# Start of an attention and expert kernel written in place, ranks in six products, first expert split later

## The chip, the cores and the metric

The program runs on one core of a Trainium2 chip. The metric is the device time of one execution in microseconds (us). The core has five engines, each with its own queue of instructions in a fixed order: TensorE (PE, matmuls), VectorE (DVE), ScalarE (ACT), GpSimd (POOL) and SyncE (SP, which mostly issues DMAs). They wait for each other through semaphores. An instruction that waits holds up everything behind it on its own engine.

## What is computed

Attention over 8 batches of 8 heads with 576 tokens and a head size of 64, in which scores below the row maximum less tau are dropped, and then a layer of 8 experts of which each token takes the best one:

```python
scores = scale * np.matmul(q, k.transpose(0, 1, 3, 2))
thresh = np.max(scores, axis=-1, keepdims=True) - tau
scores = np.where(scores >= thresh, scores, -1000000000.0)
attn = np.exp(scores - np.max(scores, axis=-1, keepdims=True))
attn = attn / (np.sum(attn, axis=-1, keepdims=True) + 1e-09)
x = np.matmul(attn, v)            # transposed to [4608, 512]
logits = x @ w_gate
expert_idx = np.argmax(logits, axis=1)
gate_w = softmax(logits)[np.arange(N), expert_idx]
for e in range(8):                # xe: the tokens of expert e
    out[expert_idx == e] = gate_w[mask, None] * (np.maximum(xe @ w1[e], 0.0) @ w2[e])
```

All in float32: q, k, v [8, 8, 576, 64], w1 [8, 512, 1024], w2 [8, 1024, 512].

## The kernel before

**Precision.** float32 operands are held as two float16 parts, `hi` (the rounded value) and `lo` (the rest), and a product takes two or three float16 matmuls.

**Pairs and steps.** The 64 heads are worked on as 32 pairs, 10 steps to a pair. In step k, `s_unit` (L276) computes a tile of scores s of a pair that is ten steps ahead, from which DVE takes row maxima (nm, L298). `parts(n)` (L301) joins these into r, PE transposes r (tile pst, L309), ACT and DVE split the result into three float16 rows (ptT, L314 to L317), and three DMAs write these rows into the operand tile CQ (L323). `st_unit` (L325) computes the transposed scores st with that CQ, so that the threshold is already subtracted; ACT takes the exponential, DVE masks it, ACT and POOL split it into ph and pl, and `av_piece` (L393) multiplies by v a pair later.

**Operands of a pair.** `load_qk` (L207) loads q and k of a pair as one tile of 128 partitions (a head in each half), `split` (L215) makes hi and lo, and `stack` (L230) copies their halves with 12 DMAs on SP (L243 to L252) into the tiles QK, ck and CQ that the matmuls read; in these the halves of the 128 partitions hold different parts of the same head. At the start this is also done for pairs 0, 1 and 2, before the first threshold rows.

**Routing.** When a batch b is done, its rows are transposed by DMAs (xTg, L499), `logits` (L513) multiplies by the gate, DVE finds the best expert, and `ranks` (L569) counts each token's place within its expert, by matmuls of 8 columns. A chain on DVE (rk to posi, L581 to L588) ends in row numbers, by which POOL sends the rows to the buffer xs (L596). The functions `tables0` to `tables2` (L1000 on) build the lists of rows for each expert (a DVE chain, all at L619, that ends in the tile `row`); `fetch` (L808) gathers rows with them (Rm, L816), and DMAs on SP transpose these (xTm, L822). `pst`, `lg`, `rk` and the tables' `pc` all use one PSUM tile (the pool `ps_m` has one buffer), so that the matmul of one waits until the one before has been read.

**Experts.** `load_w` (L763) loads 512 KB of weights on SP, `split_w` (L776) makes their hi on ACT (L782) and lo on DVE (L783), eight such pieces to an expert. The first expert has two load buffers; piece i + 2 is loaded when piece i has been split. `gemm1` (matmul L874) and `gemm2` (matmul L901) are cut into chunks, of which 0.15 of a chunk runs in each step from 304 to 320, and one in each step after.

**What sets the order.** Functions are planned for a step (`plan`, `after`), and each step writes out what is due. From `first` (step -20) to step 304 (KM) the instructions stand on every engine as they are written; the start ahead of it (loads, constants, the first pair) and everything from step 304 on are put in order by a scheduler. Before, the first expert's eight pieces are split in steps 286, 289 and so on to 307 (L1058 to L1060):

```python
    k = NSTEP * (NPAIR - 2) - LEAD - SL
    plan(k + 1, room)
    for i in range(8):
        plan(k + WS0 + WSD * i, lambda i=i: split_w(*wseq[i]))
```

## Time and profile before

| | |
|---|---|
| device time of three runs, us | 975.71, 977.86, 980.07 (median 977.86) |
| the profiled execution, us | 975.46 |
| its span, first to last instruction, us | 973.4 (2.1 lie outside it) |
| mean granted clock of TensorE in it | 0.986 |
| busy, us (share of the span) | PE 919.6 (94%), DVE 646.3 (66%), ACT 618.6 (64%), POOL 558.7 (57%) |

A profile tells for each engine when it was busy, and for its idle stretches which other engine's event or DMA ended them. The granted clock says at which part of full speed PE ran: 1.00 is 2.4 GHz, 0.50 is 1.2 GHz. Attention takes the first 571 us; what follows are the other experts.

### The profile page before, as it was taken

The page shows a single profiled execution, that of the slowest core. Times are in us where ns is not written, and L with a number is a line of the kernel's source. Part 1 is how long each engine was busy: PE and PEld are TensorE (multiplying, and loading weights), DVE is VectorE, ACT ScalarE, POOL GpSimd, SP SyncE. Part 2 cuts the span into 40 slices and gives each one's busy share as a digit, 9 for nine tenths or more (in the row PEclk, how much of TensorE's full clock was granted, in tenths as well). Part 3 has the DMA queues.
Part 4 walks back from the last instruction along what each step waited for, and adds up shares of the span by engine and source line. Part 5 has one row for each costly group of instructions (what it writes and reads, how often), then busy time and mean ns, then how long its engine had stood idle before and what let it go on. Part 6 is the DMA issues. An engine that isn't in the chain of part 4 may idle for free. (4 is left out here: it accounts for less than half of the span.)

```text
span 973.4 us, 25204 instructions
## 1 busy us (share of the span) xinstructions
PE 919.6 (94%) x10027; PEld 653.2 (67%) x10027; DVE 646.3 (66%) x1309; ACT 618.6 (64%) x1036; POOL 558.7 (57%) x477
## 2 busy tenths in 40 slices
PE   3699999999999999999988999899999999999997
PEld 1267777676777767767656787586677666677684
DVE  6698888888888888888888755735243341532650
ACT  2589898888888988988867744335333342433651
POOL 5378887998998979989957743431222212121121
PEclk9899999999999999999988999999999999999999
DMA  7554565484675765936656579998475565646720
GB/s 184 135 123 106 126 145 136 121 184 115 181 154 138 168 139 137 206 96 160 141 147 175 97 196 308 341 201 238 141 230 155 177 171 155 221 124 212 227 95 27
DMA packets 181715, 158.96 MB, mean 163 GB/s; under 512 B 137561, under 2 KB 153947, under 8 KB 181596
## 3 DMA queue, kind: packets, MB, share of 16 engines
q1 hardware_dynamic: 129244, 100.35, 42.2%
q10 hardware_dynamic: 43200, 27.53, 10.8%
q0 software_dynamic: 9152, 29.45, 9.2%
q8 instruction: 80, 1.31, 0.6%
q14 instruction: 39, 0.32, 0.1%
HBM read 90.24 MB, written 19.44 MB: 113 GB/s over the span
## 5 line engine op out<-in xcount | busy, mean ns | idle before, releaser
L372 POOL TENSOR_TENSOR pl<-e,ph 128x1024 f16<-128x1024 f32 x95 | 203.0, 2139 | 61.9 <-ACT ph L371 58.6
L298 DVE TENSOR_REDUCE nm<-s 128x1 f32<-128x512 f32 (+1 forms) x320 | 202.0, 635 | 16.6 <-PE s L288 13.5
L901 PE MATMUL y<-wb,hl 128*128 128x512 f16 (+1 forms) x1056 | 201.5, 360 | 1.3 <-DVE hl L863 1.3
L874 PEld LDWEIGHTS <-wb 128*128 128x128 f16 x2304 | 188.6, 98 | 19.9 <-issue 2.4
L874 PE MATMUL h<-xTm,wb 128*128 128x256 f16 (+2 forms) x2112 | 195.5, 253 | 1.8 <-DMA xTm<-R 1.8
L901 PEld LDWEIGHTS <-hl 128*128 128x128 f16 (+1 forms) x1056 | 94.1, 100 | 100.5 <-DVE hl L863 2.3
L783 DVE SCALAR_TENSOR_TENSOR wb<-wf,wb 128x1024 f16<-128x1024 f32 x96 | 118.6, 1269 | 56.6 <-ACT wb L782 55.0
L366 DVE SCALAR_TENSOR_TENSOR e<-st,e 128x512 f32<-128x512 f32 x192 | 129.3, 674 | 37.2 <-POOL pl L372 25.7
L363 ACT ACTIVATE e<-st,ntau 128x512 f32<-128x512 f32 x192 | 129.9, 688 | 36.9 <-PE st L336 35.0
L286 PE MATMUL s<-QK 128*128 128x512 f16 (+3 forms) x640 | 137.5, 293 | 13.9 <-DMA QK<-lo 13.6
L288 PE MATMUL s<-ck,CQ 128*128 128x512 f16 (+3 forms) x640 | 142.1, 290 | 3.3 <-DMA ck<-lo 3.3
L335 PE MATMUL st<-QK 128*128 128x512 f16 (+3 forms) x640 | 138.1, 292 | 3.2 <-DVE e L366 3.0
L336 PE MATMUL st<-CQ,ck 128*128 128x512 f16 (+3 forms) x640 | 132.7, 290 | 7.2 <-DMA CQ<-ptT 7.2
L915 POOL DMA_INDIRECT out_dram<-o,gt x40 | 43.6, 1089 | 133.6 <-ACT o L912 123.0
L782 ACT ACTIVATE wb<-wf 128x1024 f16<-128x1024 f32 x96 | 97.2, 1048 | 33.0 <-DMA wf<-in_w_dram 18.0
L414 PE MATMUL av<-vf,e 128*128 128x65 f32 (+1 forms) x1024 | 116.9, 252 | 0.0
L862 ACT ACTIVATE hl<-h 128x512 f16<-128x512 f32 (+1 forms) x80 | 45.8, 572 | 111.6 <-PE h L874 109.5
L347 ACT ACTIVATE e<-st,ntau_f 128x512 f32<-128x512 f32 (+1 forms) x160 | 94.4, 611 | 28.7 <-PE st L336 28.5
L414 PEld LDWEIGHTS av<-vf,e 128*128 128x128 f32 (+1 forms) x1024 | 102.1, 165 | 0.3
L371 ACT CAST ph<-e 128x1024 f16<-128x1024 f32 x96 | 99.4, 1036 | 3.5 <-DVE ptT L317 1.6
L418 PE MATMUL av<-vop,pl 128*128 128x65 f16 x768 | 97.5, 195 | 0.0
L417 PE MATMUL av<-vop,ph 128*128 128x64 f16 x768 | 97.4, 194 | 0.0
(203 smaller groups left out, 1490.7 us busy)
## 6 DMA issues: line engine op xcount, KB each, us to landing
wf<-in_w_dram SPq DMA_DIRECT2D x96, 512.0 KB
qkf<-in_qk_dram ACTq DMA_DIRECT2D x30, 576.0 KB
vf<-in_v_dram ACTq DMA_DIRECT2D x30, 320.0 KB
QK<-hi SPq DMA_DIRECT2D x64, 144.0 KB
QK<-hi SPq DMA_DIRECT2D x64, 72.0 KB
QK<-lo SPq DMA_DIRECT2D x64, 72.0 KB
ck<-lo SPq DMA_DIRECT2D x64, 72.0 KB
CQ<-hi SPq DMA_DIRECT2D x64, 64.0 KB
```

The source lines that it names most:

```text
L286: nc.tensor.matmul(sc[rows, oc], d["QA"][a][:, cols], d["KB"][a][:, CH[c]], start=True, stop=False)
L288: nc.tensor.matmul(sc[rows, oc], d["CQ"][:, at:at + cols.stop - cols.start], d["CK"][a][:, CH[c]], start=False, stop=True,)
L298: nc.vector.tensor_reduce(o, sc[:, 0:width(t)], axis=AX.X, op=ALU.max, negate=True)
L335: nc.tensor.matmul(sc[rows, oc], d["KB"][a][:, cols], d["QA"][a][:, CH[c]], start=True, stop=False)
L336: nc.tensor.matmul(sc[rows, oc], d["CK"][a][:, cols], d["CQ"][:, q], start=False, stop=True)
L363: nc.scalar.activation(pf, sc, AF.Exp, bias=ntau, scale=0.125 / SS)
L366: nc.vector.scalar_tensor_tensor(pf, sc, 0.0, pf, ALU.is_ge, ALU.mult)
L372: (nc.vector if (n, t) in PLV else nc.gpsimd).tensor_tensor(l, pd, h, ALU.subtract)
L414: nc.tensor.matmul(av[rows, a], d["Pf"][t][:, q], vf[:, tv], start=False, stop=last)
L783: nc.vector.scalar_tensor_tensor(o[:, :, 1], x, SW, o[:, :, 0], ALU.mult, ALU.subtract)
L874: nc.tensor.matmul(o, Wt[:, c, wh, f], x, start=c == 0 and z == 0, stop=c == 3 and z == 2,)
L901: nc.tensor.matmul(o, h[:, hh], Wt[:, f, wh, c], start=f == 0 and z == 0, stop=f == 7 and z == 2)
```

## The change

- **Start.** The order written by hand begins with the first instruction. Pair 0 is loaded twice, so that each half of the 128 partitions holds the same head (four DMAs on SP), and ACT, DVE and POOL write QK, ck and CQ of it in place (`rounded_0`, `rest_0`): its 12 copies by DMA are gone. Pair 1 is loaded on ACT's queue, split by ACT and POOL, and its 12 copies stand half on SP and half on ACT. Pair 2 is split sooner, its copies in the order hi, CQ, lo. The threshold rows of pair 0 go out on ACT's queue. Constants that nobody needs yet (iotas, memsets, the gate's weights) are held back and written five to a step on POOL and two to a step on DVE; the fourth buffer's memsets move from DVE to POOL.
- **Ranks.** A batch of n blocks takes n + 1 matmuls of up to 8 n columns in place of n (n + 3) / 2 of 8 columns: six for n = 5 (20 before), five for n = 4 (14 before).
- **First expert.** Its pieces are split in steps 300, 302, 304, 306, 309, 312, 315 and 318.
- **Logits of batch 6.** They move from step 306 to step 315, with a dependency on the last matmul of st.

```diff
--- before.py
+++ after.py
@@ start of the program, inside the order that is written by hand @@
+    for a in range(2):
+        for z in range(2):
+            nc.sync.dma_start(xds[a][64 * z:64 * z + 64], qk[0][64 * a:64 * a + 64])
+    for i in range(3):
+        fill(i, nc.vector)
+        nc.gpsimd.memset(cqs[i][64:P], 0.0)
+        if i == 0:
+            nc.scalar.copy(hqs[0][64:P, 0:1], cks[0][0][64:P, 0:1])
+            for w in range(2):
+                nc.scalar.dma_start(x1[w], qk[1][:, w])
+
+    def rounded_0(a):
+        nc.scalar.activation(hqs[a], xds[a][:, 0], AF.Copy, scale=SQ)
+        nc.scalar.activation(qks[a][:, 1], xds[a][:, 1], AF.Copy, scale=SQ)
+
+    def rest_0(a):
+        q, k = xds[a][LO, 0], xds[a][HI, 1]
+        nc.vector.scalar_tensor_tensor(qks[a][LO, 0], q, SQ, hqs[a][LO], ALU.mult, ALU.subtract)
+        nc.vector.scalar_tensor_tensor(cks[0][a][HI], k, SQ, qks[a][HI, 1], ALU.mult, ALU.subtract)
+        nc.gpsimd.tensor_copy(qks[a][HI, 0], hqs[a][HI])
+        copy = nc.gpsimd.tensor_copy if a else nc.scalar.copy
+        copy(cqs[0][HI, a * NT * P:(a + 1) * NT * P], hqs[a][HI, 0:NT * P])
+        copy(cqs[0][HI, 8 * P + 64 * a:8 * P + 64 * a + 64], hqs[a][HI, NT * P:S])
...
-    nc.gpsimd.iota(iota_i, pattern=[[1, E]], base=0, channel_multiplier=0)
+    hg.iota(iota_i, pattern=[[1, E]], base=0, channel_multiplier=0)
...
+    for w in range(2):
+        nc.scalar.activation(hi_1[:, w], x1[w], AF.Copy, scale=SQ)
+    for w in range(2):
+        nc.scalar.activation(x1[w], x1[w], AF.Copy, scale=SQ)
+        nc.gpsimd.tensor_tensor(lo_1[:, w], x1[w], hi_1[:, w], ALU.subtract)
...
+    def spread():
+        for eng, k0, w in ((hg, 3, 5), (hv, 13, 2)):
+            for i, f in enumerate(eng.ops):
+                plan(first + k0 + i // w, f)
@@ stack(n) @@
+        if n == 1:
+            for h, e in ((x, nc.sync), (y, nc.scalar)):
+                for f in first(*h) + query(*h) + low(*h):
+                    f(e)
+            return
+        if n == 2:
+            for part in first, query, low:
+                for h in heads:
+                    for f in part(*h):
+                        f(nc.sync)
+            return
@@ parts(n), rows(t) @@
-                nc.sync.dma_start(
+                (nc.sync if n else nc.scalar).dma_start(
@@ finish(b): step of the logits @@
-            d + TUNE["lg7"] if last else phase(7, d + TUNE["lg"]), lambda: logits(b, n, xTs, dist),
+            d + TUNE["lg7"] if last else phase(7, d + (14 if b == B - 2 else TUNE["lg"])), lambda: logits(b, n, xTs, dist),
...
+                if b == B - 2 and j == m == 0:
+                    tc.add_manual_dep(mm.ins, mark[0].name, SYNC)
@@ ranks() @@
-            for j in range(n):
-                nc.tensor.matmul(rkv[:, j], before, oh[:, j], start=True, stop=False)
-                for i in range(j):
-                    nc.tensor.matmul(rkv[:, j], ones, oh[:, i], start=False, stop=False)
-                nc.tensor.matmul(rkv[:, j], ones, was, start=False, stop=True)
+            nc.tensor.matmul(rkv, before, oh, start=True, stop=False)
+            for i in range(n - 1):
+                nc.tensor.matmul(
+                    rkv[:, i + 1:n], ones, oh[:, i:i + 1].to_broadcast([P, n - 1 - i, E]), start=False, stop=False
+                )
+            nc.tensor.matmul(rkv, ones, was.unsqueeze(1).to_broadcast(bc), start=False, stop=True)
@@ plans of the pairs and of the first expert @@
-            plan(max(first, k - TUNE["sp0"]), lambda n=n: split(n))
-            plan(max(first + 3, k), lambda n=n: stack(n))
+            plan(max(first + 3, k) if n > 1 else first + 2, lambda n=n: stack(n))
...
-        plan(k + WS0 + WSD * i, lambda i=i: split_w(*wseq[i]))
+        k = KEND - 2 * NSTEP + 2 * i + max(i - 3, 0)
+        plan(k, lambda i=i: split_w(*wseq[i]))
```

**SP at the start.** The threshold rows of pair 0 (`CQ<-ptT`, L323 before) stand behind the last copies of pair 2. QK, ck and CQ are the stacked operands, hi and lo the parts of a pair. Before:

```order
L243 DMA QK_1_360<-hi_307 64x1152
L244 DMA QK_1_360<-lo_308 64x576
L245 DMA QK_1_360<-hi_307 64x576
L246 DMA ck_1_158<-lo_308 64x576
L251 DMA CQ_163<-hi_307 64x512
L252 DMA CQ_163<-hi_307 64x64
L251 DMA CQ_163<-hi_307 64x512
L252 DMA CQ_163<-hi_307 64x64
L323 DMA CQ_161<-ptT_375 1x9x128 x3
L243 DMA QK_0_462<-hi_399 64x1152
```

After, they stand on ACT (L426), behind its half of pair 1's copies, the load of pair 3 and the scaling of that load:

```order
L325 DMA CQ_105<-hi_122 64x512
L326 DMA CQ_105<-hi_122 64x64
L319 DMA QK_1_229<-lo_123 64x576
L320 DMA ck_1_99<-lo_123 64x576
L281 DMA qkf_286<-in_qk_dram 128x1152
L417 ACTIVATE ptT_366<-pst_364,thr 9x128
L419 CAST ptT_366<-pst_364 9x128
L295 ACTIVATE qkf_286<-qkf_286 128x1152
L426 DMA CQ_104<-ptT_366 1x9x128 x3
```

The three rows leave SP's queue, and what stands ahead of them is one load and its scaling on ACT in place of twelve copies of pair 2.

**DVE around the end of the chain to posi**, for which pst of pair 30 waits (steps 290 to 292). wb is a piece of the first expert's weights, e the masked exponentials, nm the row maxima. Before:

```order
L305 TENSOR_REDUCE r_9564<-nm_9254 128x9
L585 TENSOR_SCALAR sm_9189<-rk_9493 128x5
L783 SCALAR_TENSOR_TENSOR wb_0_9302<-wf_1_0_9306,wb_0_9302 128x1024
L586 TENSOR_REDUCE rk_9493<-rk_9493 128x5
L348 SCALAR_TENSOR_TENSOR e_6_9536<-st_7_9556,e_6_9536 128x512
L298 TENSOR_REDUCE nm_9595<-s_0_9596 128x1
L587 RECIPROCAL sm_9189<-sm_9189 128x5
L588 CAST posi_9191<-rk_9493 128x5
```

After:

```order
L408 TENSOR_REDUCE r_9499<-nm_9207 128x9
L691 TENSOR_SCALAR sm_9142<-rk_9442 128x5
L692 TENSOR_REDUCE rk_9442<-rk_9442 128x5
L451 SCALAR_TENSOR_TENSOR e_6_9471<-st_7_9491,e_6_9471 128x512
L401 TENSOR_REDUCE nm_9526<-s_0_9527 128x1
L693 RECIPROCAL sm_9142<-sm_9142 128x5
L694 CAST posi_9144<-rk_9442 128x5
```

The split of a piece (wb) is gone from between sm and posi.

**SP in steps 302 to 306.** wf are loads of the first expert, xTg the transposed rows of batch 6, xTm those of the first expert's gathered rows Rm; CQ here belongs to the last pair. Before:

```order
L769 DMA wf_1_1_9769<-in_w_dram 128x1024
L769 DMA wf_2_1_9861<-in_w_dram 128x1024
L499 DMA_TRANSPOSE xTg_0_9863<-R_209 128x8x128 x2
L499 DMA_TRANSPOSE xTg_2_9917<-R_209 128x8x128
L769 DMA wf_3_1_9939<-in_w_dram 128x1024
L499 DMA_TRANSPOSE xTg_2_9917<-R_209 128x8x128
L323 DMA CQ_164<-ptT_9946 1x9x128 x3
L822 DMA_TRANSPOSE xTm_9957<-Rm_9956 128x8x128
```

After:

```order
L602 DMA_TRANSPOSE xTg_0_9782<-R_196 128x8x128 x2
L875 DMA wf_2_0_9838<-in_w_dram 128x1024
L602 DMA_TRANSPOSE xTg_2_9840<-R_196 128x8x128 x2
L426 DMA CQ_107<-ptT_9865 1x9x128
L875 DMA wf_3_0_9877<-in_w_dram 128x1024
L426 DMA CQ_107<-ptT_9865 1x9x128
L875 DMA wf_0_1_9952<-in_w_dram 128x1024
L928 DMA_TRANSPOSE xTm_9880<-Rm_9879 128x8x128
L426 DMA CQ_107<-ptT_9865 1x9x128
L928 DMA_TRANSPOSE xTm_10005<-Rm_10004 128x8x128
```

Three loads now stand among and ahead of the last pair's threshold rows, each of which waits until DVE has split the piece two before it, and the first xTm stands ahead of the last threshold row.

## Rows read from the trace of the kernel before

**Rows 1.** The page, part 1: busy time, share of the span and instructions of each engine.

```profile
PE 919.6 (94%) x10027; PEld 653.2 (67%) x10027; DVE 646.3 (66%) x1309; ACT 618.6 (64%) x1036; POOL 558.7 (57%) x477
```

**Rows 2.** Timeline of SP's queue at the start: start, length, then the instruction.

```profile
12.80 1.18 SPq L246 DMA_DIRECT2D ck<-lo  x2
...
24.02 0.54 SPq L243 DMA_DIRECT2D QK<-hi  x1
...
32.55 2.54 SPq L323 DMA_DIRECT2D CQ<-ptT  x3
```

**Rows 3.** Timeline of PE at the start; idle time before and its releaser in brackets.

```profile
17.50 0.58 PE L288 MATMUL s<-ck,CQ 128*128 128x512 f16 x1 [3.33 <-DMA ck<-lo]
...
25.43 0.28 PE L309 MATMUL pst<-ident,r 128*9 128x128 f32 x1 [0.83 <-DVE r L305]
...
36.29 0.59 PE L336 MATMUL st<-CQ,ck 128*128 128x512 f16 x1 [6.51 <-DMA CQ<-ptT]
```

**Rows 4.** Timeline of DVE at the start.

```profile
10.79 1.43 DVE L227 SCALAR_TENSOR_TENSOR lo<-qkf,hi 128x576 f16<-128x576 f32 x2
...
29.27 0.27 DVE L317 TENSOR_TENSOR ptT<-pst,ptT 9x128 f16<-9x128 f32 x1
```

**Rows 5.** Transfers of 0 to 40 us, in 40 slices of 1 us.

```profile
GB/s 0 0 55 160 415 401 309 242 156 180 132 66 64 138 240 373 205 154 194 331 305 181 96 31 65 157 138 136 159 235 304 303 43 0 5 2 136 166 74 9
```

**Rows 6.** Timeline of PE at a ranks batch of four blocks: first matmul, and what follows.

```profile
549.65 0.17 PE L575 MATMUL rk<-oh,before 128*128 128x8 f16 x1
...
550.08 0.41 PE L335 MATMUL st<-QK 128*64 128x512 f16 x2
```

**Rows 7.** Waits of PE, 450 to 640 us: us in total, times, longest.

```profile
PE pst L309 <- DVE row L619: 4.7, 1, 4.7
PE pst L309 <- DVE posi L588: 3.8, 1, 3.8
PE lg L519 <- DMA xTg<-R: 1.7, 1, 1.7
```

**Rows 8.** Waits of PE, 90 to 450 us.

```profile
PE pst L309 <- DVE pos L592: 1.4, 1, 1.4
```

**Rows 9.** Timeline of DVE, 484 to 556 us.

```profile
502.37 2.90 DVE L783 SCALAR_TENSOR_TENSOR wb<-wf,wb 128x1024 f16<-128x1024 f32 x1
...
523.68 1.23 DVE L783 SCALAR_TENSOR_TENSOR wb<-wf,wb 128x1024 f16<-128x1024 f32 x1 [0.75 <-ACT wb L782]
...
528.70 0.19 DVE L619 CAST row<-pc 128x32 int32<-128x32 f32 x1
```

**Rows 10.** Windows: length, busy PE, PEld, DVE, ACT, POOL, clock, DMA share, GB/s.

```profile
506.00:512.00 6.00, 5.14 (x26) 3.11 (x27) 5.10 (x11) 3.48 (x8) 1.54 (x3) 0.50 0.65 186
...
528.00:533.00 5.00, 4.05 (x33) 3.11 (x33) 4.89 (x11) 3.58 (x9) 4.68 (x4) 0.50 1.14 278
...
538.00:545.00 7.00, 6.26 (x62) 4.82 (x63) 5.27 (x9) 4.00 (x7) 4.94 (x5) 0.76 0.87 158
...
530.00:571.50 41.50, 39.77 (x611) 35.14 (x610) 26.33 (x65) 26.41 (x50) 27.69 (x23) 0.92 0.59 140
```

**Rows 11.** Timelines of POOL, SP and PE: from the row table to the first expert matmul.

```profile
534.05 1.03 POOL L816 DMA_INDIRECT Rm<-xs,row  x1 [0.79 <-DMA xTg<-R]
...
539.69 2.64 SPq L822 DMA_TRANSPOSE xTm<-Rm  x2
...
545.82 0.83 PE L874 MATMUL h<-xTm,wb 128*128 128x128 f16 x12
```

**Rows 12.** Timelines of SP and ACT: a load of the first expert and the split it feeds.

```profile
531.50 1.12 SPq L769 DMA_DIRECT2D wf<-in_w_dram  x1
...
537.82 1.06 ACT L782 ACTIVATE wb<-wf 128x1024 f16<-128x1024 f32 x1 [2.17 <-DMA wf<-in_w_dram]
```

**Rows 13.** Timeline of SP after attention, and the group of gemm2 on the page.

```profile
589.65 20.53 SPq L769 DMA_DIRECT2D wf<-in_w_dram  x13
...
L901 PE MATMUL y<-wb,hl 128*128 128x512 f16 (+1 forms) x1056 | 201.5, 360 | 1.3 <-DVE hl L863 1.3
```

More of the change, by code (lines that the diff above doesn't have):

```diff
@@ L81 @@
     pp = apool.enter_context(tc.tile_pool(name="pp", bufs=5))
+    order = ExitStack()
+    order.enter_context(tc.manual_schedule(engines={
+        mybir.EngineType.PE, mybir.EngineType.DVE, mybir.EngineType.Activation, mybir.EngineType.Pool,
+        mybir.EngineType.SP,
+    }))
+    NM = 3
+    KC = 64 + NM
+    NB = 3
+    NQ = 4
+    NV = 6
+    cks = [[cpool.tile([P, S], F16, name=f"ck_{i}_{a}") for a in range(2)] for i in range(NQ)]
+    cqs = [op.tile([P, 9 * P], F16, tag=f"CQ{i}", name=f"CQ_{i}", bufs=1) for i in range(NQ)]
@@ new lines, with fill, wide @@
+    vops = [cpool.tile([P, NV, 2 * D + 1], F16, name=f"vop_{i}") for i in range(NB)]
+    vfs = [cpool.tile([P, 10, D + 1], F32, name=f"vf_{i}") for i in range(NB)]
+    def fill(i, eng):
+        for a in range(2):
+            eng.memset(cks[i][a][64:P], 0.0)
+            eng.memset(cks[i][a][64:KC], 1.0)
+    def wide(pool, dt, tag, name):
+        return pool.tile([P, 2, 512], dt, tag=tag, name=name).rearrange("p a c -> p (a c)")[:, 0:S]
+    xds = [ld.tile([P, 2, S], F32, tag="qkf", name=f"x_{a}") for a in range(2)]
@@ new lines @@
+    hqs = [wide(pp, F16, "ph", f"hq_{a}") for a in range(2)]
+    qks = [op.tile([P, 2, S], F16, tag=f"QK{a}", name=f"QK_0_{a}") for a in range(2)]
+    x1 = [wide(ew, F32, "e", f"x1_{w}") for w in range(2)]
+    hi_1, lo_1 = (ld.tile([P, 2, S], F16, tag=z, name=f"{z}_1") for z in ("hi", "lo"))
+    for a in range(2):
+        for z in range(2):
[7 more added lines that the diff above has]
+                nc.scalar.dma_start(x1[w], qk[1][:, w])
@@ L138 @@
+    hv.tensor_scalar(lanes[:, 1:2], upper, -float(P2), float(P), ALU.mult, ALU.add)
+    hv.tensor_tensor(lanes[:, 1:2], lanes[:, 1:2], lane, ALU.add)
     run = cpool.tile([P, E], F16, name="run")
-    nc.gpsimd.memset(run, 0.0)
+    hg.memset(run, 0.0)
+    rounded_0(0)
+    rest_0(0)
+    rounded_0(1)
+    rest_0(1)
+    for f in hn.ops:
+        f()
+    for w in range(2):
[3 more added lines that the diff above has]
+        nc.gpsimd.tensor_tensor(lo_1[:, w], x1[w], hi_1[:, w], ALU.subtract)
@@ L143 @@
+    hg.memset(cqs[3][64:P], 0.0)
+    fill(3, hg)
+    for i in range(NB):
+        hg.memset(vops[i][:, :, D:D + 1], SV / SX)
+        hg.memset(vfs[i][:, 0:8, D:D + 1], 1.0 / SX)
+        for a in range(2):
+            hg.memset(vfs[i][64 * a:64 * a + 64, 8 + a, D:D + 1], 1.0 / SX)
+            hg.memset(vfs[i][64 - 64 * a:128 - 64 * a, 8 + a, D:D + 1], 0.0)
     REST, CORNER = 9, 10
     WHOLE = (6, 7, 8, REST, CORNER)
-    NV = 6
-    NM = 3
-    KC = 64 + NM
-    NB = 3
-    NQ = 4
-    cks = [[cpool.tile([P, S], F16, name=f"ck_{i}_{a}") for a in range(2)] for i in range(NQ)]
@@ L212, in load_v, with split @@
         (nc.scalar if n >= 2 else nc.sync).dma_start(vfs[n % NB][:, :, 0:D], v[n // 2][:, n % 2])
-    def split(n, lag=1):
+    def split(n):
         d = st[n]
@@ L219, in split @@
         d["lo"] = lo = ld.tile([P, 2, S], F16, tag="lo", name=f"lo_{n}")
[L220 to L227 removed]
+        if n == 2:
+            nc.scalar.activation(hi, x, AF.Copy, scale=SQ)
+        nc.scalar.activation(x, x, AF.Copy, scale=SQ)
+        if n > 2:
+            after(1, lambda: nc.scalar.copy(hi, x))
+        after(2 if n > 2 else 0, lambda: nc.gpsimd.tensor_tensor(lo, x, hi, ALU.subtract))
     def stack(n):
@@ L335, in st_unit @@
             nc.tensor.matmul(sc[rows, oc], d["KB"][a][:, cols], d["QA"][a][:, CH[c]], start=True, stop=False)
-            nc.tensor.matmul(sc[rows, oc], d["CK"][a][:, cols], d["CQ"][:, q], start=False, stop=True)
+            mark[0] = nc.tensor.matmul(sc[rows, oc], d["CK"][a][:, cols], d["CQ"][:, q], start=False, stop=True).ins
         sc = sc[:, 0:w]
@@ L1180, in one_step @@
             k += 1
-        with tc.manual_schedule(engines={mybir.EngineType.PE, mybir.EngineType.DVE, mybir.EngineType.Activation, mybir.EngineType.Pool, mybir.EngineType.SP}):
-            while k < KM:
-                one_step()
+        while k < KM:
+            one_step()
+        order.close()
         while busy:
```

124 lines of the change are left out of this document (64 added, 60 removed).

## The prediction

> **What bounds the kernel now.** I read the page's shares first: PE is busy for 919.6 of 973.4 us, so the end is set by PE, and only two things shorten it: PE's idle time (53.8 us) and matmuls that PE needn't do or does at half clock [rows 1]. Next I read PE's own timeline and waits for where that idle time lies. At the start, PE's second matmul begins at 17.50, and at 36.29 it has waited 6.51 for the threshold rows of pair 0 [rows 3]; from there on it is nearly always busy. The other places are late: 3.8 us of pst for posi and 4.7 us of pst for `row` [rows 7]. Last I read the clock: after each of these two waits a stretch runs at 0.50, which is 1.2 GHz in place of 2.4 [rows 10]. So I cost three places, the start, 500 to 571, and what comes right after, and take what lies between as it is: there the changed program has the same order on every engine but for the ranks.
>
> **The start (gain 10, between 7 and 12).** The chain before: DVE makes pair 0's lo from 10.79 to 12.22 [rows 4], SP copies it from 12.80, PE can use it at 17.50 [rows 2, 3], which is 4.7 after the issue; pst follows at 25.43 [rows 3], the last part of ptT ends at 29.54 [rows 4], 4.1 later. Then the three threshold rows wait until 32.55, since twelve copies of pair 2 stand ahead on SP, the first at 24.02: 3.0 us; their issue takes 2.54 [rows 2] and PE goes on at 36.29, 1.2 after the last issue.
> In the changed program pair 0's lo needs no copy. DVE starts on it later than data would allow, because twelve memsets and four small operations come first, where sixteen and eight did before; by that share of the 10.79 us I estimate 8, and the two halves that the first tile needs take 1.4 (1.43 for two [rows 4]). PE's first full tile is then at about 9.5, against 17.50. The stage to pst took 7.9 (17.50 to 25.43), so pair 0 alone would allow pst at 17.4. But two tiles of pair 1 stand ahead of pst on PE, and pair 1's lo is still copied: it is ready on POOL at about 12.5, my estimate, the time at which pair 0's was before, and with the same 4.7 it arrives at 17.2. Both agree: pst at 17.5. Add 4.1 for ptT, 2.54 for the issue, 1.2 for the landing: 25.3, if the 3.0 us of waiting on the queue go. On ACT the rows now stand behind the load of pair 3 and its scaling, for which there is no row; from below it costs nothing (the load is issued well before pst), from above the 3.0 us that SP cost. I take 1. So 36.3 becomes 26.3: 10 us; ends are 7 (3.0 on the queue, pst 1 late) and 12 (no wait, pst 1 earlier). PE still waits some 3 us there, so the stretch at low clock stays. The constants held back (about 15 operations on DVE, 70 on POOL) go beside pair 1's tiles, while PE waits for threshold rows anyway; without that cover they would cost the same 1 us that I allow.
> The doubled loads bring 0.59 MB more. The slices of 4 to 6 us moved 415 and 401 GB/s [rows 5], so that is about 1.5 us of the transfers, and it is hidden as long as DVE's memsets last to 8. The Trainium skill says in "DMA: Bandwidth & Descriptors", Rules for kernel authors, that two transfers to disjoint partition halves serialize and that one transfer of 128 partitions is to be used. By it the doubling costs its 1.5 us of transfer in full and the sum would be 1.5 smaller at worst; the trace has no such pair of loads.
>
> **Ranks (gain 2.2, between 0 and 2.8).** A batch of four blocks takes 14 matmuls from 549.65 to 550.08, 0.031 each [rows 6]. There are 36 blocks in 4 batches of four and 4 of five: 4 x 14 + 4 x 20 = 136 matmuls before and 4 x 5 + 4 x 6 = 44 after. 92 x 0.031 = 2.8; the remaining ones are up to 40 columns wide, and I take 2.2.
>
> **Step 290 to 295 (gain 5, between 2.4 and 6.4).** DVE's 2.90 us split stands in the chain to posi [rows 9], for which pst waits 3.8 [rows 7]. The split is gone; what is late next is the chain itself, which in an undisturbed batch still makes pst wait 1.4 [rows 8]. So the wait falls by 2.4. In 506 to 512 PE works 5.14 us at clock 0.50 [rows 10]; at full clock this is 2.6 less, if the short wait no longer draws it. 2.4 + 2.6 = 5.0; only the wait: 2.4; no wait at all: 6.4.
>
> **Step 302 to 311 (gain 0, between -6 and +6).** Lost here before: 4.7 at pst and 1.7 at the logits [rows 7], half of 4.05 busy at 0.50 (2.0), and 0.24 of 6.26 (1.5) [rows 10]: 9.9. Gone with the change: one split of 1.23 and its wait of 0.75 in the chain to `row` [rows 9], so that pst waits 2.7, and the logits, which move behind the last st. What is late next is the first expert's input. `row` is ready at 528.89 [rows 9], POOL's gather starts at 534.05, SP transposes from 539.69, 10.8 after `row`, and PE uses the result at 545.82, 16.9 after it, without waiting [rows 11]. PE's way from pst to that matmul is shorter by the logits and the low clock: 16.9 less 2.8 less 3.5 is 10.6. A transpose takes 1.3 to issue (2.64 for two [rows 11]), so xTm is usable between 12 and 16.9 after `row`; PE waits 1.4 to 6.3, say 4. The last of the three threshold rows of the last pair now stands behind that transpose on SP, and behind three loads which wait for DVE's splits, so it comes no sooner. With 2.5 of low clock after it: 2.7 + 4 + 2.5 = 9.2, against 9.9. I call this 0; the ends are a wait of 1.4 with no low clock after it (+6) and 4.7 at pst again with 6.3 and 5 of low clock (-6). The eight splits run in here as well (about 1.0 on ACT and 1.2 on DVE each); ACT is busy 26.4 of 41.5 [rows 10], so 5 more fit as a sum.
>
> **After attention (loss 4, between 0 and 11).** Thirteen loads of experts stand ahead of the transposes of the next group, six before. Thirteen take 20.53 on SP [rows 13], 1.58 each, so seven take 11. PE has 34 matmuls of earlier groups in reserve there, 201.5/1056 = 0.19 each [rows 13]: 6.5. 11 - 6.5 is 4.5; I take 4.
>
> **Sum.** 10 + 2.2 + 5 + 0 - 4 = 13.2. The profiled execution took 975.46 (973.4 of span and 2.06 outside it): 962.3. The timed runs' median is 977.86, 2.4 above it; by that it is 964.7. I forecast 963.
>
> **Rivals.**
> *The start gives little: 969.* ACT's queue holds the threshold rows as SP's did, and pair 1's lo arrives late, so that the gain is 4. For it: the rows wait behind a load of 576 KB. Against: that load is issued before pst even begins. The Trainium skill ("DMA: Bandwidth & Descriptors", Issuing engines are not separate DMA queues) says that issuing from several engines saves only the sequencer's time, which is usually small. By it this rival is what happens; rows 2 speak against "small" here, since 3.0 us of waiting stand between ptT and its issue.
> *All late stalls go: 949.* 3.8 + 4.7 + 1.7 of waits, 6.1 of clock, and nothing lost after attention: 16.3 + 12.2 = 28.5 off 977.9. Against: the chain from `row` to xTm is not shortened by anything.
> *The late part takes it back: 975.* The two last terms near their ends, -5 and -9 in place of 0 and -4, leave 17.2 - 14 = 3 us.
> *Slower, 987: ACT is held by the loads of its splits.* With two buffers each of the last six loads starts after a split. A load issued at 531.50 lets ACT go on at 537.82 [rows 12], 6.3 later; ACT's exponentials of the last two pairs stand behind each. Six waits of 5.3 are 32 us; ACT has 41.5 - 26.4 - 5 = 10 to spare [rows 10], so PE loses 22: 977.9 - 13.2 + 22 = 987. It decides the sign from 4.7 us a load on: six of them less 10 are the 18 that outweigh 13.2 by 0.5%. For it: ACT's second and third split stand next to each other. Against: the loads overlap in pairs, and PSUM lets PE run five tiles ahead.
>
> **Chances.** Forecast 0.55, small start 0.15, no late stalls 0.12, taken back 0.11, slower 0.07. About 0.5% is what a measurement can tell from no change here: below 973 is faster (0.82), to 982.7 the same (0.11), above it slower (0.07). The range of 8 in 10 goes from 950 to 974.
>
> **What would show it.** The first wait for `CQ<-ptT` ends near 26 (right between 24 and 29); pst's wait for posi is at 1.4 or less, with clock 1.00 behind it; PE's longest wait between 510 and 560 is at the first matmul of gemm1, for xTm, or at st for `CQ<-ptT`; after attention h or y waits 2 to 6 us. Wrong would be: ACT waiting over 4 us for wf several times before the end of attention, or the first CQ landing after 30.

## The result, and the profile after

The changed kernel takes 963.0 us (median of 4 runs, 960.84 to 965.12), beside 976.79 for the kernel before on the same chip (974.15 to 980.07): a ratio of 0.9857, 95% interval 0.9827 to 0.9887. The forecast was 963. The profiled execution took 965.12, the longest of the four, with a span of 963.3, which is 10.1 less than that of before; the medians are 13.8 apart. The sums below are of the profiled pair.

The page, part 1 (busy time, share of the span, instructions), beside [rows 1]:

```profile
PE 918.3 (95%) x9935; PEld 652.4 (68%) x9935; DVE 646.6 (67%) x1307; ACT 622.0 (65%) x1043; POOL 561.2 (58%) x486
```

PE has 92 matmuls fewer in the trace and almost the same busy time; what went is idle time (53.8 us before, 45.0 after). Where it went is read from four moments that both traces have: pst of pair 29 (the last one that both reach without a wait of over 0.5), pst of pair 31, the last av (the start of its last group of four matmuls), and the end.

| stretch, us | before | after | won |
|---|---|---|---|
| start to pst of pair 29 | 486.03 | 478.31 | 7.7 |
| to pst of pair 31 | 42.92 | 34.81 | 8.1 |
| to the last av | 41.93 | 45.14 | -3.2 |
| to the end of the span | 402.5 | 405.0 | -2.5 |

In the three later stretches PE's idle time went from 9.1, 1.7 and 3.1 us to 4.6, 4.9 and 4.5, and its mean granted clock from 0.89, 0.91 and 1.00 to 1.00, 0.93 and 0.99.

**Start.** PE's timeline (start, length, instruction, idle time before with its releaser), the answer to [rows 3]:

```profile
9.50 0.58 PE L389 MATMUL s<-QK 128*128 128x512 f16 x1 [9.50 <-DVE QK L132]
...
12.28 0.63 PE L389 MATMUL s<-QK 128*128 128x512 f16 x1
12.70 0.63 PE L391 MATMUL s<-ck,CQ 128*128 128x512 f16 x1
...
15.26 0.26 PE L391 MATMUL s<-ck,CQ 128*64 128x64 f16 x1 [0.99 <-POOL CQ L137]
...
21.49 0.38 PE L389 MATMUL s<-QK 128*128 128x512 f16 x1
21.71 0.38 PE L391 MATMUL s<-ck,CQ 128*128 128x512 f16 x1
21.96 0.28 PE L412 MATMUL pst<-ident,r 128*9 128x128 f32 x1
...
30.48 0.38 PE L439 MATMUL st<-CQ,ck 128*128 128x512 f16 x1 [2.92 <-DMA CQ<-ptT]
```

The first tile starts at 9.50, as forecast; pst comes at 21.96 and not at 17.5, and the first st with threshold rows at 30.48 and not at 26.3. ACT's timeline of the same stretch tells why pst is late and what holds the rows (ACTq is ACT's DMA queue):

```profile
6.01 0.68 ACT L127 ACTIVATE hq<-x 128x576 f16<-128x576 f32 x1 [3.72 <-DMA x<-in_qk_dram]
...
11.95 0.68 ACT L127 ACTIVATE hq<-x 128x576 f16<-128x576 f32 x1 [4.03 <-DMA x<-in_qk_dram]
...
24.58 0.26 ACT L419 CAST ptT<-pst 9x128 f16<-9x128 f32 x1 [1.95 <-DVE pst L418]
26.23 1.16 ACT L295 ACTIVATE qkf<-qkf 128x1152 f32<-128x1152 f32 x1 [1.40 <-DMA qkf<-in_qk_dram]
26.30 2.97 ACTq L426 DMA_DIRECT2D CQ<-ptT  x3
```

The second head of pair 0 has landed only at 11.95, and the rows are issued right behind the scaling of pair 3, which waits for its load.

**End of attention and after it.** PE's waits from 440 to 640 us (total, times, longest), the answer to [rows 7]:

```profile
PE pst L412 <- DVE row L725: 4.6, 1, 4.6
PE pc L1087 <- DVE posi L694: 3.3, 1, 3.3
PE h L980 <- DMA xTm<-Rm: 3.2, 1, 3.2
PE st L438 <- DVE e L469: 3.0, 2, 1.7
PE h L980 <- DMA R<-R: 0.6, 1, 0.6
```

pst's wait for posi is gone and so is the logits' wait; pst's wait for `row` is as long as before; h for xTm and pc for posi are new. The windows (length; busy time and count of PE, PEld, DVE, ACT, POOL; granted clock; DMA share; GB/s) show the clock falling behind three of them, pst's wait, the second of st's and pc's; behind the wait for xTm it stays at 1.00 (528 to 540):

```profile
510.00:515.00 5.00, 1.88 (x13) 1.39 (x14) 4.23 (x5) 2.06 (x5) 4.68 (x5) 0.79 0.69 136
540.00:545.00 5.00, 5.00 (x62) 4.63 (x60) 5.00 (x10) 4.58 (x9) 3.90 (x3) 0.66 0.38 108
585.00:590.00 5.00, 2.47 (x25) 2.40 (x26) 4.38 (x20) 1.24 (x3) 3.23 (x3) 0.80 1.12 302
```

### The profile page after: what moved, and what is told of

It reads as the page before. It is cut to its first block, busy times and chain, and to the rows that moved or that the text cites. A ratio compares the mean times of both kernels' runs of the same rounds, so it can differ in the third digit from the quotient of the medians.

```text
span 963.3 us, 25013 instructions
## 1 busy us (share of the span) xinstructions
PE 918.3 (95%) x9935; PEld 652.4 (68%) x9935; DVE 646.6 (67%) x1307; ACT 622.0 (65%) x1043; POOL 561.2 (58%) x486
## 5 line engine op out<-in xcount | busy, mean ns | idle before, releaser
L888 ACT ACTIVATE wb<-wf 128x1024 f16<-128x1024 f32 x96 | 97.6, 1050 | 27.9 <-PE h L980 10.0
L451 DVE SCALAR_TENSOR_TENSOR e<-st,e 128x512 f32<-128x512 f32 (+1 forms) x160 | 91.2, 586 | 8.8 <-ACT e L450 7.7
```

## The experiments

Twelve kernels ran. The columns: median (runs), ratio to the kernel before on the same chip with its interval, and from the profiled execution the first st with threshold rows and the four stretches of the table above.

| kernel | us (runs) | ratio | first st | to pst 29 | to pst 31 | to last av | to end |
|---|---|---|---|---|---|---|---|
| before | 976.79 (4) | 1 | 36.29 | 486.0 | 42.9 | 41.9 | 402.5 |
| after | 963.00 (4) | 0.9857 [0.9827, 0.9887] | 30.48 | 478.3 | 34.8 | 45.1 | 405.0 |
| ranks alone | 979.71 (10) | 1.0021 [0.9995, 1.0047] | 36.67 | 485.9 | 42.0 | 45.0 | 403.1 |
| splits back | 976.73 (10) | 1.0000 [0.9985, 1.0015] | 29.32 | 475.6 | 41.7 | 46.0 | 408.1 |
| old start | 978.07 (10) | 1.0013 [0.9994, 1.0031] | 37.30 | 484.7 | 34.8 | 44.1 | 412.0 |
| logits back | 971.19 (10) | 0.9912 [0.9887, 0.9937] | 30.32 | 479.1 | 34.8 | 44.4 | 411.5 |
| v later | 971.53 (10) | 0.9953 [0.9930, 0.9975] | 31.43 | 479.9 | 34.8 | 45.0 | 409.4 |
| whole loads | 973.14 (1) | | 30.37 | 479.8 | 34.8 | 45.2 | 411.2 |
| rows first | 965.27 (6) | 0.9896 [0.9863, 0.9930] | 29.27 | 479.1 | 34.8 | 43.4 | 406.1 |
| whole loads, rows first | 961.95 (1) | | 28.80 | 476.8 | 34.8 | 43.5 | 405.2 |
| two early | 965.62 (4) | 0.9872 [0.9847, 0.9896] | 29.83 | 478.2 | 33.2 | 42.9 | 409.8 |
| two early, logits back | 970.66 (4) | 0.9899 [0.9857, 0.9941] | 30.93 | 481.3 | 33.2 | 44.6 | 412.8 |
| pc_2 of its own | 964.83 (8) | 0.9897 [0.9867, 0.9926] | 29.54 | 476.6 | 34.8 | 42.9 | 407.4 |
| three edits | 962.84 (4) | 0.9858 [0.9819, 0.9898] | 28.82 | 479.1 | 33.2 | 42.1 | 410.1 |

Each row's moments come from one execution. After and the five kernels whose start is the same (splits back, logits back, two early, two early with logits back, pc_2 of its own) have their first st between 29.3 and 30.9 and pst of pair 3 between 60.6 and 64.5, so differences of a us or two in these columns are not to be relied on.

### One part alone, or one part undone

**Ranks alone**: the kernel before with the new ranks and nothing else of the change (the hunk at `rkv` in the diff).

> The kernel before with the new ranks alone. Theory (92 matmuls fewer, at 0.02 to 0.03 us each): the threshold product of pair 29 comes 1.9 us sooner, 975. Rival (the ranks' matmuls lie in gaps where PE waits for the next threshold anyway): no shift, 976.8.

No gain: the end lies within 0.5% of before, and pst of pair 29 comes 0.1 us sooner. A batch's ranks do get shorter (from the first matmul to what follows, 0.50 to 0.15 us for five blocks and 0.36 to 0.13 for four), which is 1.4 us for the five batches ahead of that pst. In this trace the waits of pst for DVE's chain (run, pos and posi), from 40 to 486 us, take the gain up: they are 6.8 in all, 4.5 before. Old start (below), with the same order on PE, DVE, POOL and SP up to there, has 4.4 and reaches that pst 1.3 sooner than before. So one profiled execution doesn't tell how much of the 1.4 is kept; the timed runs of ranks alone show none. And the stretch from pst of pair 31 to the last av takes 45.0 without any later split in it, which is what it takes after (here st waits 3.3 for gt, which DVE makes of the gathered rows). So the -3.2 of the table can't be put down to the splits from this alone: a kernel without them can lose as much there.

**Splits back**: the changed kernel with the eight splits at their old steps.

```diff
-        k = KEND - 2 * NSTEP + 2 * i + max(i - 3, 0)
+        k = NSTEP * (NPAIR - 2) - LEAD - SL + 6 + 3 * i
```

> The changed kernel with the first expert's eight splits back at steps 286, 289 to 307; all else as changed. Theory (the later splits gave the 8 us that the changed kernel wins between the thresholds of pair 29 and pair 31, by leaving DVE's chain to posi, and cost 3 us after that): pst of pair 30 waits about 4 us for posi again, the clock behind it is 0.50, the first expert matmul does not wait for xTm; in sum about 968 against 963 for the changed kernel. Rival (the gain there is a by-product of the earlier start and of the shorter ranks): no wait of pst for posi over 1 us, 963.

Its waits of PE from 440 to 640 us:

```profile
PE st L438 <- DVE gt L933: 4.5, 1, 4.5
PE pst L412 <- DVE row L725: 4.5, 1, 4.5
PE pst L412 <- DVE posi L694: 3.9, 1, 3.9
```

The wait for posi is back at 3.9 as in [rows 7], and the stretch to pst of pair 31 goes from 34.8 to 41.7: the move of the splits is worth 6.9 there, of which 4.8 are idle time of PE and 1.8 its low clock. The stretch that the splits were moved into is not shorter without them (46.0). The whole gain of the change is gone with this one edit (976.7, where 968 was expected), more than the 6.9: the stretch after attention is 3 longer too.

**Old start**: the kernel before with the ranks, the later splits and the later logits of the change, without the new start.

> The kernel before with the new ranks, the later splits and the later logits of batch 6, but with the old start. Theory (the start is worth what its threshold rows came sooner, 5.8 us, and 6.7 by the fourth pair, and none of it is given back): 969.5. Rival A (the start's 10 us of the prediction are there, but partly lost elsewhere): 973. Rival B (what starts earlier only waits later): 964.

First st at 37.30 and pst of pair 29 at 484.7, 6.4 later than after: that is what the start is worth. Pst of pair 31 follows in the same 34.8, and the last av is 5.4 later than after. So the start holds most of its gain up to the last av; and yet the end is that of before, above all three expected times, since the stretch after attention takes 412.0. Against before, the last av comes 7.3 sooner and 9.5 are lost behind it. But the changed kernel, whose last av is sooner still, takes 405.0 there. The 7.0 between the two are 5.0 of PE's idle time and 1.7 of its low clock; why the old start brings them isn't known.

### What sets the first st

**v later**: the first load of v planned behind pair 1's copies, so that it takes no part of the transfers at the start.

```diff
-        load_v(0)
-        work = experts()
+        work = experts()
...
-        if n:
-            plan(max(first, NSTEP * n + TUNE["lv"]), lambda n=n: load_v(n))
+        plan(max(first, NSTEP * n + TUNE["lv"]) if n else first + 3, lambda n=n: load_v(n))
```

> The changed kernel with the load of v for pair 0 (320 KB in packets of 256 bytes) moved on SP from behind the gate's weights to behind pair 1's copies. Theory 1 (that load shares the DMA engines with the second head of pair 0, which lands at 11.95 and holds the first stage): ACT's first operation on the second head at 9 to 10, pst of pair 0 at 19.5 instead of 21.96, 960.5. Theory 2 (the four loads of 64 partitions and pair 1's own loads are slow by themselves): the second head still lands after 11, 963.

The second head is usable on ACT at 11.73 in place of 11.95, the first st comes at 31.43, no sooner. The load of v isn't what delays it. The kernel as a whole is slower than the changed one (0.9953), mostly after attention (409.4).

**Whole loads**: pair 0's four loads onto 64 partitions replaced by two onto 128.

```diff
-        for z in range(2):
-            nc.sync.dma_start(xds[a][64 * z:64 * z + 64], qk[0][64 * a:64 * a + 64])
+        nc.sync.dma_start(xds[a], qk[0])
```

> The changed kernel with pair 0's four loads of 64 partitions replaced by two of 128 partitions with the same bytes; each then holds both heads, so that pair 0 computes with the wrong rows, and nothing else changes. Theory (transfers to 64 partitions move only half as fast, which is why the second head lands at 11.95 where before 1.18 MB had landed by 7.3): the second tile's first operation on ACT at 8 to 9, the first st with thresholds at 27 to 28. Rival (the loads share the engines with pair 1's, which are issued meanwhile): second tile at 11 or later, first st at 30 to 31.

ACT's timeline:

```profile
4.74 0.68 ACT L126 ACTIVATE hq<-x 128x576 f16<-128x576 f32 x1 [2.44 <-DMA x<-in_qk_dram]
...
6.55 0.68 ACT L126 ACTIVATE hq<-x 128x576 f16<-128x576 f32 x1
...
26.20 1.16 ACT L294 ACTIVATE qkf<-qkf 128x1152 f32<-128x1152 f32 x1 [3.18 <-DMA qkf<-in_qk_dram]
26.26 2.97 ACTq L425 DMA_DIRECT2D CQ<-ptT  x3
```

The same bytes land 5.4 us sooner for the second head (6.55 against 11.95), pst comes at 19.72, and the first st at 30.37, as without this edit: ACT now waits 3.18 for pair 3's load, and the rows go out at the same time. So there are two limits in a row. Of the whole loads the Trainium skill says in "DMA: Bandwidth & Descriptors", Rules for kernel authors, that two transfers to disjoint partition halves serialize and one transfer of 128 partitions is to be used. This run agrees that the whole transfer is the faster one, by the 5.4 us; it doesn't show whether the halves ran one after the other.

**Rows first**: in the changed kernel the scaling of pair 3 two steps later, behind the threshold rows on ACT's queue.

```diff
-            plan(max(first + 1, k - TUNE["sp0"]) if n > 2 else first + 1, lambda n=n: split(n))
+            plan(max(first + 1, k - TUNE["sp0"] + (2 if n == 3 else 0)) if n > 2 else first + 1, lambda n=n: split(n))
```

> The changed kernel with one edit: the scaling of pair 3 is planned two steps later, so that on ACT's queue the three threshold rows of pair 0 stand ahead of it and not behind it. In the kernel after, ACT waits there for pair 3's load until 26.23, the rows are issued from 26.30 to 29.27, and the first st runs at 30.48; ptT's first two parts were ready before 24.9, its third at 27.3. Theory (ACT's queue holds the rows): the first two rows go out from 24.9, the third at 27.3, and the first st runs at about 29.3, 1.2 sooner; 962 at the end, if what is won at the start is kept. Rival (the third part of ptT sets the time, and the issue is no limit): first st unchanged within 0.4.

ACT's queue issues the rows as soon as ptT's parts are there, and PE goes on at 29.27:

```profile
24.33 0.26 ACT L419 CAST ptT<-pst 9x128 f16<-9x128 f32 x1 [1.95 <-DVE pst L418]
24.39 3.42 ACTq L426 DMA_DIRECT2D CQ<-ptT  x3
```

From pst to that st it takes 7.6, where the changed kernel and the five others with its start took 8.5 to 9.9. So ACT's queue did hold the rows, for 1 to 2 us. No trace of it is left further on: pair 1's own threshold rows are next, and PE waits 2.3 for them at 44.95, with the clock at 0.50 from 46 to 48. Pst of pair 3 is at 63.54, within the 60.6 to 64.5 of the kernels without this edit, and the time is 965.3.

**Whole loads, rows first**: both edits.

> The edit of the run with pair 0's rows loaded as two whole transfers of 128 partitions (both tiles then hold the heads mixed, so pair 0's rows are not the reference's), and besides it the threshold rows of pair 0 ahead of pair 3's scaling on ACT. Loads alone left the first st at 30.37, with ptT ready at 25.8. Theory (two limits in a row, the 64-partition loads and then ACT's queue): only both edits together move it, to about 27.7. Rival (something else, such as pair 1's copies on ACT's and SP's queue, lands no sooner): still 29 or more.

The first st comes at 28.80, 1.7 before that of the changed kernel and not 2.8: between 21.1 and 27.9 the clock is at 0.53 in the mean, and PE comes to this tile of st only at 28.39, with nothing idle ahead. Ahead of that work PE has waited 1.75, to 22.82, for the copy of pair 1's lo, which is what the rival named. So a third limit stands behind the two, pair 1's copies and PE's own work at 1.2 GHz. That both edits go further than rows first alone isn't shown: three edits (below), with the start of rows first, has its first st at 28.82.

### What becomes of the time after pst of pair 31

**Two early**: two of the splits ahead of the chain to `row`, three behind.

```diff
-        k = KEND - 2 * NSTEP + 2 * i + max(i - 3, 0)
+        k = (293, 295, 303, 305, 309, 312, 315, 318)[i]
...
-            plan(k, lambda i=i: load_w(*wseq[i + 2]))
+            plan((299, 303, 303, 305, 309, 312)[i], lambda i=i: load_w(*wseq[i + 2]))
```

> The changed kernel with the first expert's first two splits at steps 293 and 295 (they were at 300 and 302), the third and fourth at 303 and 305, and their loads at 299 and 303. Theory (the split of 3.09 us in DVE's chain to the row table holds pst of pair 31, and through the load behind it on SP also the transposes for which the gather waits): pst waits 1.5 instead of 4.6, the first expert matmul 0 to 1 instead of 3.2 for xTm, less at low clock; 957. Rival (both waits come from the length of the chain and of the gather): both waits stay within 1 us of what they were, 962 to 964.

Pst waits 2.5 for `row` in place of 4.6, which agrees with the split that the timeline of after shows in that chain (below); h still waits 2.6 for xTm, where 0 to 1 was expected. The last av comes at 554.37, 3.9 sooner, and the end is where it was.

**Logits back**: the logits of batch 6 at their old step.

```diff
-            d + TUNE["lg7"] if last else phase(7, d + (14 if b == B - 2 else TUNE["lg"])), lambda: logits(b, n, xTs, dist),
+            d + TUNE["lg7"] if last else phase(7, d + TUNE["lg"]), lambda: logits(b, n, xTs, dist),
```

> The changed kernel with the logits of batch 6 back at step 306 and without their dependency on the last st. Theory (the later logits make the row lists of the second expert's groups late, so that their transposes stand behind thirteen loads on SP, and the scheduler puts the last pc product ahead of work that could cover it: this is what PE loses after attention): from the last av to the end 402 to 403 us in place of 405.0, at the price of up to 1.7 us of wait for xTg at the logits; 960 to 962. Rival (the waits after attention come from batch 7's own chain): 405 from the last av to the end, 963 to 965.

Slower, though the logits of batch 6 don't wait: the loss lies after attention. The logits of batch 7 wait 2.6 and 2.1 for xTg, and h waits 3.9 for xTm. **Two early, logits back** puts both edits together.

> The kernel of e4b_two_early with the logits of batch 6 back at step 306. Theory (e4b wins 3.5 us up to the last av and loses 4.5 after it, and the loss comes with the late logits): last av near 555, 403 from there to the end, 959. Rival (what is won up to the last av is lost after it whatever the logits do): 409 from the last av on, 965.

It is slower again, by 7.7 in the profiled execution, with one wait that is longer than this loss:

```profile
PE h L978 <- DMA xTm<-R: 11.4, 1, 11.4
```

So the later logits are no cost; by the ratios they are worth some 5 us in the changed kernel. The 3 of two early lie within the intervals.

**pc_2 of its own**: the PSUM tile of the third count from another pool, so that its matmul needn't wait until posi is read.

```diff
-        ps = ps_m.tile([P, 512], F32, tag="m", name=f"pc_{nm}")
+        ps = (ps_av if i == 2 else ps_m).tile([P, 512], F32, tag="av" if i == 2 else "m", name=f"pc_{nm}")
```

> The changed kernel with one edit: the PSUM tile of the third count (pc_2) is taken from the pool of the y tiles in place of the one buffer that rk, pc, lg and pst share, so that its matmul no longer waits until posi has been read out of rk. In the kernel after, PE waits 3.3 us there (pc for posi, at 586.9) and works 3.4 us at clock 0.50 from 588.0 on. Theory (that wait is the loss after attention, term -4 of the sum): the wait and the low clock go, 3.3 + 1.7 = 5 us, 958. Rival (the transposes of the next group come 11.5 us later after the last av than before, and h of the next group takes the wait over): PE waits 2 to 4 us at h for the transposes of R instead, 961 to 963.

PE's longest waits from 554 us on:

```profile
PE h L980 <- DMA R<-R: 3.4, 1, 3.4
PE rk L679 <- DVE run L659: 1.6, 1, 1.6
```

The wait for posi is gone, and h's wait for the transposes of R has taken its place: 0.6 has become 3.4. That is the rival, though the time is 964.8 and not its 961 to 963.

**Three edits**: rows first, two early and pc_2 of its own.

> The changed kernel with three edits together: the threshold rows of pair 0 ahead of pair 3's scaling on ACT, two of the eight splits one and two steps earlier than the row chain (splits at 293, 295, 303, 305, 309, 312, 315, 318; this alone ended attention 3.5 us sooner and gave it back later), and pc_2 in a PSUM buffer of its own. Theory (each of these waits was worth its length, and what was given back after attention was pc_2's wait): 1.2 + 3.5 + 5 us, about 953 to 955. Rival (after attention the transfers of the next groups set the pace whatever comes before): 960 to 965, with waits at h for transposes of R.

It is level with the changed kernel (intervals of the two ratios nearly the same), though the last av comes at 554.44. That is the rival again. Its waits from 554 us on begin with:

```profile
PE h L980 <- DMA R<-R: 4.2, 1, 4.2
PE y L1007 <- DVE hl L969: 3.0, 1, 3.0
```

**What these runs say together.** SP's queue after attention in the kernel before (not shown ahead) and in the changed one:

```profile
582.45 1.80 SPq L769 DMA_DIRECT2D wf<-in_w_dram  x2
584.42 5.19 SPq L822 DMA_TRANSPOSE R<-R  x2
```

```profile
568.31 14.78 SPq L875 DMA_DIRECT2D wf<-in_w_dram  x9
583.27 3.31 SPq L928 DMA_TRANSPOSE R<-R  x2
```

Two loads of experts stood directly ahead of R's transposes, now there are nine, and they hold SP for 14.8 us. R's transposes begin 13.5 after the last av before and 25.0 after it now. The first h of R runs 29.5 after the last av in the changed kernel, and 29.5, 29.9, 30.0, 30.0, 30.5, 30.5 and 31.4 in v later, rows first, whole loads, whole loads with rows first, three edits, pc_2 of its own and two early. PE's idle time from the last av up to that h is 3.9 to 5.4 in all eight, whichever instruction the waits are put down to. Splits back and old start have the nine loads too, with 30.8 and 33.0, and 5.3 and 6.9 idle. So what comes sooner at the last av moves SP's stretch along with it, but a wait that is taken away inside of it is given back at h.

No run moved the nine loads by themselves. The two kernels with the logits back do it by the way: R's transposes stand ahead of these loads, and the first h of R runs 26.9 and 20.2 after the last av, but then 17 loads stand ahead of the next transposes (xTm of R), for which h waits 3.9 and 11.4. In logits back:

```profile
558.98 3.65 SPq L926 DMA_TRANSPOSE R<-R  x2
...
572.42 29.76 SPq L873 DMA_DIRECT2D wf<-in_w_dram  x17
603.02 3.73 SPq L926 DMA_TRANSPOSE xTm<-R  x1
```

That fits the queue as the cause, but in these two the order on other engines differs as well, so the cause is made likely and not shown.

One thing holds for all eleven kernels that differ from the changed one by an edit or by a part undone: their stretch from the last av to the end is longer than its 405.0, by up to 7.8. So a part of the changed kernel's time may lie in how the waits of this one order happen to fall, and not in any one part of the change.

Beyond that h, the eight kernels still differ by up to 6 us (375 to 381 from that h to the end). A part is waits at y for the next results (2.3 and 3.0 in two early and three edits) and the clock. Another part, 3.4 us in whole loads and 3.7 in v later, is short gaps between the matmuls of h, which the trace puts down to no releaser ("issue"), and of which the changed kernel has none with the same order. In v later:

```profile
PE h L980 <- issue: 3.7, 8, 1.1
```

I don't know their cause. Single executions of one kernel also differ by up to 9 us (963.51 to 972.47 for pc_2 of its own), so differences of 2 to 3 us between kernels in that column are not to be relied on.

## Why the time was right and the terms were not

The sum was 13.2 on the profiled execution. That pair shows 10.1 in the span, the medians 13.8. That the median meets the 963 to the us is luck: the forecast lies between two bases that are 2.4 apart, and the terms are off by over 3 each way. The terms, one by one:

**Start: 10 forecast, 5.8 at the first st, 6.4 to 6.7 kept.** The step that failed is the stage from the first tile to pst, which was taken over with its 7.9 us. It took 12.5 (pst at 21.96, and at 20.5 to 21.0 in the five other kernels with this start). Three things in it differ from [rows 3]. The second head lands at 11.95, and PE waits 0.4 and 1.0 for the operands made of it, until 15.3. PE works at half speed nearly to its end, with matmuls of 512 columns 0.43 apart to 21.2 and 0.22 from 21.5 on; in the kernel before they were 0.43 apart only from 17.88 to 20.0, and 0.22 from 21.85. And DVE starts on the row maxima only at 14.78, since the second head's lo stands ahead of them in its order; with both heads early (whole loads) they start at 13.27 and end by 19.49. The second path was late with it: pair 1's lo was to be ready on POOL at 12.5 and to arrive at 17.2, but POOL starts on it at 15.18, behind the second head's copies, and SP issues its copies only at 16.91 and 17.71. The first tile (9.5; DVE's start at 8 was 7.2 by the share of all operations named there, and is 8.60) and the sum from pst to the first st (8.8 forecast, 8.5 measured) were right, though inside of that ptT got longer, from 4.1 to 5.4. DVE's timeline shows it. The two operations that make ptT's third part were 1.6 apart before (27.69, and 29.27 in [rows 4]) and are 2.8 apart now, with constants that were held back between them (a cast of 8 columns takes 0.97 here, 0.17 before, while POOL writes its held memsets from 22.69 to 25.41):

```profile
24.21 0.34 DVE L418 SCALAR_TENSOR_TENSOR pst<-pst,thr,ptT 9x128 f32<-9x128 f32 x1
24.47 0.97 DVE L146 CAST iota_e<-iota_i 128x8 f32<-128x8 int32 x1
25.47 0.60 DVE L146 TENSOR_SCALAR rank<-iota_e 128x8 f32<-128x8 f32 x1
...
27.04 0.27 DVE L420 TENSOR_TENSOR ptT<-pst,ptT 9x128 f16<-9x128 f32 x1
```

The cover that I named for them, PE's wait for the rows, was not a cover: they stand in the chain that makes the rows. The doubled loads were 1.5 us and hidden by my count, at the rate of [rows 5]. Loaded as halves they cost 5.4 at the second head against the same bytes loaded whole. The windows of after show half of that rate at the same DMA share (408 GB/s at 1.03 from 4 to 6 us before):

```profile
4.00:6.00 2.00, 0.00 (x0) 0.00 (x0) 1.30 (x5) 0.00 (x0) 0.97 (x5) 1.00 1.01 211
6.00:8.00 2.00, 0.00 (x0) 0.00 (x0) 1.66 (x4) 1.91 (x4) 0.65 (x1) 1.00 1.00 209
```

The rival of a small start (gain 4, by ACT's queue) had the right place and half of the cause: ACT's queue holds the rows, but for 1 to 2 us. The Trainium skill ("DMA: Bandwidth & Descriptors", Issuing engines are not separate DMA queues) calls the time on the issuing sequencer usually small beside the DMA itself. The 1 to 2 us of rows first are not such a time but a wait behind ACT's activation; the issue of the three rows took 2.97 on ACT and 2.54 on SP.

**Ranks: 2.2 forecast; in the traces 0.1 to 1.3 up to pst of pair 29** (ranks alone 0.1, old start 1.3; in the changed kernel the lead over before grows by 1.1 from pst of pair 11 on). The size per batch was right: 0.23 for four blocks and 0.35 for five make 2.3 for the eight, and five of them stand ahead of that pst. Whether it can be charged to the path in full, as I did, stays open: old start and the changed kernel show nearly the full price up to that pst, while in ranks alone pst's waits for DVE grow by 2.3 and the timed runs show no gain.

**Steps 290 to 295: 5 forecast, 8.1 measured; splits back puts it at 6.9.** The mechanism was right, the size was not: I left 1.4 of the wait; none was left (pst of pair 30 starts at 493.86 with no idle time before it), and with the wait the whole stretch at 0.50 went. 3.8 and half of the stretch from 505.4 to 512.2 are 7.2. The 8.1 is the whole way to pst of pair 31, so pst's wait for `row` belongs to it too; with the 2.0 that the next term took off that wait, 7.0 were forecast for this way.

**Steps 302 to 311: 0 forecast, -3.2 measured from pst of pair 31 on** (without those 2.0 the terms of this step come to -1.3). Pst was to wait 2.7 for `row` and waits 4.55. The step that failed: I counted one split out of the chain to `row` and didn't look for one that the move puts into it. It is there, with a length that no median gives:

```profile
509.27 0.26 DVE L725 SCALAR_TENSOR_TENSOR pc<-pc,pos,has 128x32 f32<-128x32 f32 x1
509.59 3.09 DVE L889 SCALAR_TENSOR_TENSOR wb<-wf,wb 128x1024 f16<-128x1024 f32 x1
512.60 0.25 DVE L725 TENSOR_SCALAR pc<-pc,pos 128x32 f32<-128x32 f32 x1
512.88 0.19 DVE L725 CAST row<-pc 128x32 int32<-128x32 f32 x1
```

POOL's timeline tells why it took 3.09 and not 1.22. Two of POOL's operations run back to back, and the split ends 1.1 after the second:

```profile
508.60 2.13 POOL L475 TENSOR_TENSOR pl<-e,ph 128x1024 f16<-128x1024 f32 x1
510.69 0.90 POOL L360 TENSOR_TENSOR vop<-full,vop 128x384 f16<-128x384 f32 x1
```

The same holds in every trace of this case. Of 1344 splits on DVE, 59 begin while such a TENSOR_TENSOR on POOL is under way (those of one column, gt, left out). They take up to 6.09, and each ends 1.08 to 1.16 after that operation (48 of them) or after one that follows it (11, this one among them). The other 1285 take 1.17 to 1.28. So the price of a split in a chain of DVE depends on what stands on POOL beside it, and the 2.90 of [rows 9] was such a price too.

The wait for xTm was found in place and nearly in size, 3.19 for 4, and 15.2 after `row`, inside the 12 to 16.9:

```profile
528.27 0.40 PE L980 MATMUL h<-xTm,wb 128*128 128x128 f16 x4 [3.19 <-DMA xTm<-Rm]
```

The 2.5 of low clock behind it did not come (1.00 from 528 to 540). In the changed kernel the -3.2 is idle time: 3.2 for xTm and 1.7 of st for e, where before there were 1.7 of the logits. But ranks alone lost 3.0 in that stretch with no wait for xTm, and what the stretch costs varies from 41.9 to 46.0 between kernels.

**After attention: -4 forecast, -2.5 measured.** Seven more loads ahead of the transposes (nine for two, where I counted thirteen for six), 11 us by my count, 13.0 by the queue's rows. The loss at h shows in pc_2 of its own (3.4) and in three edits (4.2). In the changed kernel itself most of it stands under another name, pc's wait of 3.3 for posi, and h waits only 0.6. In all, idle time grew by 1.4, and low clock took 1.6 more.

```profile
586.91 0.18 PE L1087 MATMUL pc<-run,ones 128*128 128x8 f16 x1 [3.26 <-DVE posi L694]
587.71 0.59 PE L980 MATMUL h<-R,wb 128*128 128x128 f16 x6 [0.62 <-DMA R<-R]
```

**The rivals.** ACT was not held by the loads of its splits: it waits 8.8 us in 8 pieces for wf from 470 to 640, the longest 2.5, and the four within attention are at most 0.56. That not all late stalls would go was right, for the reason given. So the time came out by two gains too large, by 3 to 4 and by about 1, one too small by 3, and two losses that came to 5.7 where 4 stood.

## What to carry to other kernels

Before a step is moved, list what it moves into: the split that left one chain went into the next (and beside POOL's operations, where it takes over twice its time), and the loads that left one stretch went ahead of the transposes on SP's queue. Where several waits seem to end in one DMA queue, taking away one of them can bring the next one up to the same time, so follow the queue and not the instruction that waits. The ends alone can mislead: without the start, or without the later splits, the whole is as slow as before, though each is worth some 5 us at the last av. So compare moments on the way too, and take several executions before reading a us or two.

## What the runs showed of the hardware

- Four loads onto 64 partitions took much longer than two onto 128 with the same bytes: the second head was usable on ACT at 11.95 against 6.55. The halves moved 209 to 211 GB/s between 4 and 8 us at a DMA share of 1.0, the whole loads of the kernel before 408 from 4 to 6 at 1.03.
- PE's first matmuls run at half speed though the clock column reads 1.00 there: 512 columns are 0.43 apart from 9.5 to 21.2 and 0.22 from 21.5. The column's 0.50 later on (513.30 to 513.73) goes with the same 0.43.
- A split on DVE (SCALAR_TENSOR_TENSOR, 128x1024) that begins while POOL runs a TENSOR_TENSOR ends 1.08 to 1.16 after that operation of POOL or one that follows it: 3.09 at 509.59 in place of 1.22, and so in all 59 such cases of the fourteen traces.
